# Where 36 weight loads are unpacked in an attention and mixer kernel: eight per head pair in the first batch instead of six, four instead of twelve in the second, and the tail's gap in a shared tile

## The chip, the cores and the metric

The kernel runs on one core of one Trainium2 chip. The metric is device time in microseconds: the median of three runs, 1661.66 us (1660.54 to 1661.77). One further execution was taken by the hardware profiler; all rows come from it.

A core has a matrix engine (TensorE, PE in the profile; PEld is its weight load), a vector engine (VectorE, DVE), an activation engine (ScalarE, ACT), a general engine (GpSimd, POOL) and a queue that issues transfers (SyncE, SP). Each engine works through its own instructions in order and waits on semaphores for the others.

## What is computed

```python
B, H, S, D = 8, 8, 576, 64;  top_k = 32
scores = q @ k^T / sqrt(D)                  # per head, 576 x 576
kth    = the 32nd largest score of each row
scores = where(scores >= kth, scores, -1e9)
attn   = softmax(scores);  o = attn @ v
x  = o laid out as (B, S, 512)
xt = x.transpose(0, 2, 1)                   # mixer, low rank 32
u  = x + (xt @ U @ V).transpose(0, 2, 1)
out = u + relu(u @ w_ch1) @ w_ch2           # 512 -> 2048 -> 512
```

q, k and v are float32. U, V, w_ch1 and w_ch2 come in as float64. The kernel reads them as pairs of 32-bit words and makes float32 of them on the chip.

## The kernel before

**Steps.** Eight batches of four head pairs each. The 576 rows of a pair are four tiles of 128 and a tail of 64 rows, with both heads of the tail in one tile. In the first batch (pairs g = 0 to 3) the tail is a step of its own, so a pair has five steps, t = 0 to 4. From pair 4 on (`NPAIR` = 4) the tail shares the step of t = 3, and a pair has four steps. That makes 20 + 28 × 4 = 132 steps, numbered n; `ALONE` = 20 is the first step of the second batch.

**What one step does.** `scores` multiplies q and k on PE (L350) and ScalarE copies the result to SBUF, into the tile `Ssb` or, for a tail, `Stail` (L395, L404 to L406, L415, L418). `front` finds the 32 largest of each row on VectorE with four rounds of MAX8 and MATCH_REPLACE8 (L521, L534, L539). From pair 5 on, `fold` and `split` first sort each row's two halves into the larger and the smaller of two scores, with two POOL operations (L446, L449) and one of VectorE (L448), so that VectorE handles half the width; L448 needs the copied scores of the next step, and L502, L500 of the next step need L449.

Then scores below the 32nd are pushed down. A "pooled" lane does it with two POOL operations (L544, L545). A "gap" lane does it with ScalarE and POOL: L565 scales the 32nd largest, L571 writes max(0, (32nd − score) × 2^96) into a tile, and POOL subtracts this from the scores (L572). In the second and later batches a step has two gap lanes, and the step with the tail three, written in the order head 1, head 0, tail. ScalarE then takes the exponential and its row sum (L453; L582 finishes the sums).

The probabilities are transposed, by PE (`turns`, L634, L639, with copies L635, L640) for pairs 0 to 5 and by VectorE with a transfer through DRAM (`blocks`, L598, and `back`, L613) from pair 6 on. `values` multiplies them with v (L708, L711, L682) and ScalarE copies the result (L720). `mixed` scales and mixes a finished pair with U and V on PE (L750, L761, L773, L785), POOL writing the result uT (L740, L743, L801).

**The order of the work.** It is written out by hand in the loop over n, as calls of generators; no scheduler moves anything. `fill` emits matmuls of the running batch's two dense layers (`mlp`, L845 and L862, with ScalarE evictions L857 and L873) by a budget per call, so PE does the layers of one batch during the attention of the next. Each batch's layers begin when its last pair is mixed, those of batch 0 at step 20. The last batch's layers are done at the end by a multiplication scheme with fewer products (`closing`).

**The weights.** `params` lists 36 pieces: four for U and V, 16 for w_ch1, 16 for w_ch2. `next_params(1)` moves a three-stage pipeline by one: it emits the ScalarE passes still outstanding, joins the piece before last, splits the last piece, and issues the transfer of the next one (L157 on SP, 512 KB, into one of three `raw` buffers). A split queues three ScalarE passes (L179, L180, L183), of which each `fill` emits one. A join (`f64_join`) is one shift on VectorE and two additions on POOL (L203, L205). The shift is of one of two forms: the plain one with one input (L202), or, if fewer than `LATE` pieces were left when the piece was split, one with two tensor inputs (L193).

In the first batch `next_params(1)` stands in the middle of steps t = 0, 1, 2 and at the end of steps t = 0, 1, 3. From step 21 on it stands near the beginning of every step, and in the middle of steps t = 0, 1, 2. Step 19 has none, step 20 one.

**Tiles and buffers.** The pool `attn` gives a tile by tag, with a number of buffers: asking for a tile means waiting until the use of the buffer's previous tile is over. Tag `E` has two buffers; it holds the gaps of heads 1 and 0 and the POOL mask of the pooled lane. Tag `tplace` has one buffer; it holds the work copy of the tail's scores in the rounds and, in the kernel before, the tail's gap.

Line numbers below are those of the profile of the kernel before.

Of the kernel before, what the change touches and what calls it, by code (L numbers as in the profile page):

```python
# [8 lines left out]
F32 = mybir.dt.float32  # L9
# [17 lines left out]
def kernel(  # L27
# [29 lines left out]
    B, H, S, D = q.shape  # L57
    P = 128
# [4 lines left out]
    NT, TAIL = 4, 64  # L63
# [3 lines left out]
    NPAIR = H // 2  # L67
# [15 lines left out]
    attn = ctx.enter_context(tc.tile_pool(name="attn", bufs=2))  # L83
# [56 lines left out]
        return slice(h * D, (h + 1) * D)  # L140

    SLAB = 512
    LATE = 12
    spare = []


# [13 lines left out]
    def f64_parts(raw, out):  # L160
# [23 lines left out]
        ))  # L184
        return hi, bits, low, len(params) < LATE

    def f64_join(hi, bits, low, late, outs):

        if late:
            none = nought if len(bits.shape) == 2 else nought.rearrange("p o -> p o ()")
            nc.vector.scalar_tensor_tensor(  # L193
                out=bits,
                in0=bits,
                scalar=3,
                in1=none.to_broadcast(list(bits.shape)),
                op0=ALU.logical_shift_left,
                op1=ALU.bitwise_or,
            )  # L200
        else:
            nc.vector.tensor_single_scalar(bits, bits, 3, ALU.logical_shift_left)  # L202
        nc.gpsimd.tensor_tensor(bits, bits, hi, ALU.add)  # L203
        for dst, form in outs:
            nc.gpsimd.tensor_tensor(dst.bitcast(U32), form(bits), form(low), ALU.add)  # L205
# [26 lines left out]
    def next_params(n):  # L232

        while passes:
            passes.pop(0)()
        while parts:
            f64_join(*parts.pop(0))
        while raws:
            r, outs = raws.pop(0)
            if isinstance(outs, list):  # L240
                parts.append((*f64_parts(r, None), outs))
                continue
            made = f64_parts(r, outs)
            parts.append((*made, [(made[1], same)]))
        for _ in range(min(n, len(params))):
            srcs, outs = params.pop()
            raws.append((f64_raw(srcs), outs))
# [6 lines left out]
    def load(g):  # L254

        list(loading(g))
# [211 lines left out]
    def front(tiles):  # L468
# [72 lines left out]
        for c, chunk, total, _, way in lanes:  # L541
            if way == "pooled":
                gap = attn.tile([P, S], F32, tag="E", name="E")
# [17 lines left out]
        if gaps:  # L561
            slots = [lane[0] for lane in gaps]
            lo, hi = min(slots), max(slots) + 1
            least = small.tile([P, 3], F32, tag="least", name="least", bufs=3)
            nc.scalar.mul(least[:, lo:hi], m8[:, lo:hi, 7], WIDEN)  # L565
            for c, chunk, *_ in gaps:
                if c == 2:
                    gap = attn.tile([P, S], F32, tag="tplace", name="E", bufs=1)
                else:
                    gap = attn.tile([P, S], F32, tag="E", name="E")  # L570
                nc.scalar.activation(gap, chunk, AF.Relu, bias=least[:, c : c + 1], scale=-WIDEN)  # L571
                nc.gpsimd.tensor_tensor(chunk, chunk, gap, ALU.subtract)  # L572
            yield
# [593 lines left out]
    def fill(k=1):  # L1167


        nonlocal due  # L1170
        for _ in range(k):
            if passes:
                passes.pop(0)()
            if mixing and next(mixing[0], True):
                mixing.pop(0)
            due += share * (LONG if len(tiles(n)) > 1 else 1) * (EARLY if n <= ALONE + BATCH + 2 else 1)
            while due > 0:
                if not fillers:
                    due = 0.0
                    break  # L1180
                done = next(fillers[0], None)
                if done is None:
                    fillers.pop(0)
                elif not done:
                    due = 0.0
                else:
                    due -= done
# [24 lines left out]
    t = 0  # L1212
# [5 lines left out]
    for n in range(STEPS + 2):  # L1218
        if n < STEPS:
            g, t = steps[n][0]  # L1220
            if t == 0 and g < NPAIR:
                load(g + 1)
            if t == (1 if g < NPAIR else 2) and g + 1 < NP:
                ready = prep(g + 1)
            fronts[n] = front(steps[n])
            next(fronts[n])
        else:
            t = NT
        here, last = fronts.get(n, iter(())), fronts.pop(n - 1, iter(()))
        if n >= ALONE - 1 and n <= ALONE:  # L1230

            if n < ALONE:
                next(last)
                values(*steps[n - 3][0])
                list(turning)
                next(here)
                next(last)
                scores(*steps[n + 1][0])
                fold(*steps[n + 1][0])
                values(*steps[n - 2][0])  # L1240
            list(turns(*steps[n - 1][0]))
            values(*steps[n - 1][0])
            if n < ALONE:
                split(*steps[n + 1][0])
                next(here)
                next(here)
                inverse(g, 0, 2 * NT)
                mixing.append(mixed(g, 1))
                fill()
                next(here)  # L1250
                continue
            fill()
            scores(*steps[n + 1][0])
            fold(*steps[n + 1][0])
            next(here)
            while mixing:
                fill()
            next_params(1)
            fill()
            next(last, None)  # L1260
            next(here)
            fill()
            split(*steps[n + 1][0])
            next(here)
            coming = loading(g + 1)
            next(coming)
            next(coming)
            next(here)
            fill()
            continue  # L1270
        if n < ALONE:
            ease = n > 0 and eased(*steps[n - 1][0])
            if ease:
                next(last, None)
            scores(*steps[n + 1][0])
            fold(*steps[n + 1][0])
            if n >= 3:
                values(*steps[n - 3][0])
                if (n - 3) % CH == NT:
                    mixing.append(mixed((n - 3) // CH, 3))  # L1280
            list(turning)
            fill()
            next(here)
            if t < NT - 1:
                next_params(1)
            fill()
            next(ready, None)
            next(here)
            next(last, None)
            fill()  # L1290
            split(*steps[n + 1][0])
            next(here)
            if t in (0, 1, NT - 1):
                next_params(1)
            next(here)
            fill()
            if n >= 1:
                turning = turns(*steps[n - 1][0])
            continue
        next(last, None)  # L1300
        fill()
        if ALONE <= n - 3 <= STEPS - 3:
            weighted(n - 3)
            if waiting:
                waiting.clear()
                if next(mixing[0], True):
                    mixing.pop(0)
        for tile_ in tiles(n + 1):
            if tile_[1] < NT:
                scores(*tile_, len(tiles(n + 1)) > 1)  # L1310
            fold(*tile_)
        next_params(1)
        turn()
        fill()
        turn()
        next(last, None)
        for tile_ in tiles(n - 2):
            back(*tile_)
        fill()
        turn()  # L1320
        fill()
        next(last, None)
        if n < STEPS and n - 2 >= ALONE and len(tiles(n - 2)) > 1:
            scale(steps[n - 2][0][0])
        next(here, None)
        fill()
        if n >= STEPS:
            if n == STEPS:
                inverse(NP - 1, 0, 2 * NT + 1)
                scale(NP - 1)  # L1330
            weighted(n - 2)
        next(here, None)
        for tile_ in tiles(n + 1):
            split(*tile_)
        if t < NT - 1:
            next_params(1)
        fill()
        next(here, None)
        for tile_ in tiles(n - 1):
            if shared(*tile_):  # L1340
                blocks(*tile_)
        turning = turned(n - 1)
        if n < STEPS and n - 1 >= ALONE and len(tiles(n - 1)) > 1:
            inverse(steps[n - 1][0][0], 0, 2 * NT + 1)
        if n < STEPS:
            if t == NT - 1:
                coming = loading(g + 2) if g + 2 < NP else iter(())
            next(coming, None)
        next(ready, None)
        next(here, None)  # L1350
        fill()
        fill()
# [35 lines left out]
```

## Time and profile before

| | |
|---|---|
| median of three runs | 1661.66 us |
| profiled execution | 1663.47 us, its span 1661.4 us |
| PE busy | 1562.3 us (94%) |
| VectorE busy | 1550.0 us (93%) |
| ScalarE busy | 991.2 us (60%) |
| POOL busy | 1012.4 us (61%) |
| mean granted PE clock | 0.966 |
| plain shifts L202, late shifts L193 | 24 from 20.9 to 203.5 us; 12 from 210.7 to 290.7 us |

A page of the profile lists busy time by engine, the span in slices, the chain of work that ended last, and groups of instructions by source line with the idle time before them and what ended it. Answers of the trace give the same for a stretch, and single instructions in order of time. A name such as `uT<-up` reads "tile uT, written from tile up". A busy PE need not be a PE at its peak, since matmuls overlap and their ends are modelled. Where a wait has several causes, the one that came last is named.

The first batch takes the first 199 us. Step 23, the first with a tail, ends at 250 us on VectorE; its step is the longest, 18.7 us, since pair 4 is not folded.

### The profile page before, as it was taken

Reading aid. Unit: us, or ns where it says so; the run is one execution under the profiler, and the core shown is the slowest. Engines: PE = TensorE matmul, PEld = TensorE weight load, DVE = VectorE, ACT = ScalarE, POOL = GpSimd, SP = SyncE. Lnnn points to the kernel's source line nnn. Section 1 sums busy time; section 2 is a strip of 40 time slices with the busy share of each in tenths; the row PEclk is TensorE's granted clock in tenths of the full one; section 3 lists DMA queues with packets and bytes.
Section 4 is the critical chain, followed back from the end, with each engine's and each line's share of the span. In section 5 each row is a group of like instructions: output and inputs, shape, how many; then the busy total and the mean of one; then the engine's idle time right before and its main releaser. Section 6 shows DMA issues by size and latency. Waiting matters only on the chain.

```text
span 1661.4 us, 30244 instructions
## 1 busy us (share of the span) xinstructions
PE 1562.3 (94%) x9638; PEld 1188.0 (72%) x9638; DVE 1550.0 (93%) x4394; ACT 991.2 (60%) x2475; POOL 1012.4 (61%) x881
## 2 busy tenths in 40 slices
PE   4676698999899999999999999999999999999999
PEld 2444466787677887778777887788777877788776
DVE  7999999999999999999999999999999999994452
ACT  4888778665555666566665656566665656564320
POOL 4787669666656565666666565656666565653620
PEclk7777798999999999999999999999999999999999
DMA  3323232244545555454445555454545455543001
GB/s 88 90 82 94 67 95 74 57 128 128 136 126 140 139 144 138 133 138 131 129 130 137 132 152 133 131 138 129 131 128 140 129 154 132 134 123 110 8 2 29
DMA packets 280399, 189.42 MB, mean 114 GB/s; under 512 B 174288, under 2 KB 261168, under 8 KB 280240
## 3 DMA queue, kind: packets, MB, share of 16 engines
q1 hardware_dynamic: 259728, 117.62, 29.3%
q10 hardware_dynamic: 20512, 69.87, 13.3%
q8 instruction: 76, 1.25, 0.3%
q14 instruction: 83, 0.68, 0.1%
HBM read 116.49 MB, written 70.91 MB: 113 GB/s over the span
## 4 chain that ended last, share of the span: by engine, by line
PE 69%; DVE 20%; DMA 3%; POOL 3%; ACT 2%; SPq 2%; issue 1%; ACTq 0%; DVEq 0%; POOLq 0%
PE mm L862 22%; PE mm L845 19%; DVE m L539 7%; PE sc L350 6%; DVE upper L534 6%; PE O L711 6%; PE mm L938 3%; DVE first L521 2%; PE tp L938 2%; PE sc L938 2%; PE sc L382 2%; PE up L785 2%; DVE y L598 1%; PE O L708 1%; DVE place L534 1%
## 5 line engine op out<-in xcount | busy, mean ns | idle before, releaser
L845 PE MATMUL mm<-uT,w 128*128 128x320 f32 (+1 forms) x1792 | 465.3, 411 | 3.0 <-POOL uT L801 2.3
L862 PE MATMUL mm<-hT,w 128*128 128x320 f32 (+1 forms) x1792 | 462.0, 409 | 0.0
L572 POOL TENSOR_TENSOR Ssb<-Ssb,E 128x576 f32<-128x576 f32 x243 | 341.3, 1424 | 195.2 <-ACT E L571 195.2
L845 PEld LDWEIGHTS mm<-uT,w 128*128 128x128 f32 x1792 | 335.7, 192 | 104.2 <-issue 12.8
L862 PEld LDWEIGHTS mm<-hT,w 128*128 128x128 f32 x1792 | 333.6, 191 | 92.6 <-issue 11.1
L539 DVE MAX8 m<-upper 128x8 f32<-128x304 f32 (+1 forms) x774 | 362.7, 509 | 0.7
L534 DVE MATCH_REPLACE8 upper<-m,upper 128x304 f32<-128x304 f32 (+1 forms) x516 | 256.8, 505 | 0.0
L446 POOL TENSOR_TENSOR lower<-Ssb 128x576 uint32<-128x576 uint32 x108 | 152.8, 1415 | 133.3 <-ACT Ssb L395 71.3
L449 POOL TENSOR_TENSOR lower<-lower,upper 128x576 uint32<-128x576 uint32 x108 | 152.3, 1410 | 130.2 <-DVE upper L448 128.0
L453 ACT ACTIVATE Ssb<-Ssb,nmax 128x576 f32<-128x576 f32 x258 | 201.7, 784 | 19.4 <-POOL Ssb L545 9.8
L350 PE MATMUL sc<-qkT 64*128 64x288 f32 (+1 forms) x1056 | 177.7, 459 | 9.8 <-ACT Ssb L404 7.9
L571 ACT ACTIVATE E<-Ssb,least 128x576 f32<-128x576 f32 x243 | 176.2, 768 | 4.3
L502 DVE MAX8 upper<-lower 128x8 f32<-128x288 f32 x432 | 172.0, 439 | 4.4 <-POOL lower L449 4.4
L395 ACT COPY Ssb<-sc 128x576 f32<-128x576 f32 x216 | 127.5, 642 | 75.7 <-PE sc L350 75.7
L598 DVE STREAM_TRANSPOSE y<-Ssb 128x512 f32<-128x512 f32 (+1 forms) x312 | 154.1, 545 | 0.3 <-ACT Ssb L453 0.2
L711 PE MATMUL O<-PT,va 128*64 128x128 f32 x2048 | 143.8, 284 | 0.0
L857 ACT ACTIVATE hT<-mm 128x320 f32<-128x320 f32 (+1 forms) x224 | 91.1, 408 | 81.7 <-PE mm L845 77.5
L350 PEld LDWEIGHTS sc<-qkT 64*128 64x128 f32 (+1 forms) x1056 | 95.7, 197 | 50.1 <-issue 17.5
L711 PEld LDWEIGHTS O<-PT,va 128*64 128x64 f32 x2048 | 112.6, 140 | 16.1 <-issue 1.6
L720 ACT COPY XT<-O 128x128 f32<-128x128 f32 x128 | 34.0, 266 | 113.1 <-PE O L711 108.3
L534 DVE MATCH_REPLACE8 upper<-first,upper 128x304 f32<-128x304 f32 x216 | 97.5, 459 | 0.0
L500 DVE MATCH_REPLACE8 lower<-upper,lower 128x288 f32<-128x288 f32 x216 | 94.0, 443 | 0.0
(268 smaller groups left out, 2271.6 us busy)
## 6 DMA issues: line engine op xcount, KB each, us to landing
away<-y SPq DMA_DIRECT2D x416, 144.0 KB
PT<-away ACTq DMA_DIRECT2D x104, 576.0 KB
raw<-in_moe_w_ch_dram SPq DMA_DIRECT2D x32, 512.0 KB
va<-in_v_dram SPq DMA_DIRECT2D x64, 128.0 KB
scale<-rd ACTq DMA_DIRECT2D x56, 144.0 KB
out_dram<-ob SPq DMA_DIRECT2D x59, 128.0 KB
ld<-in_q_dram SPq DMA_DIRECT2D x108, 64.0 KB
ld<-in_k_dram SPq DMA_DIRECT2D x108, 64.0 KB
```

Source lines behind the costliest of these rows:

```text
L350: nc.tensor.matmul(out, lhsT=qkT[half(h), 0, cols(t)], rhs=qkT[half(h), 1, lo:hi], start=True, stop=True,)
L446: nc.gpsimd.tensor_tensor(bottom, a.bitcast(U32), b.bitcast(U32), ALU.add)
L453: nc.scalar.activation(E, chunk, AF.Exp, bias=nmax, scale=SCALE, accum_out=total)
L502: nc.vector.max(spot, lower)
L534: nc.vector.match_replace(nxt, ms[c], curs[c], NEG)
L539: nc.vector.max(ms[c], curs[c])
L571: nc.scalar.activation(gap, chunk, AF.Relu, bias=least[:, c : c + 1], scale=-WIDEN)
L572: nc.gpsimd.tensor_tensor(chunk, chunk, gap, ALU.subtract)
L598: nc.vector.transpose(y[:, :, i * NT : i * NT + c].rearrange("p r c j -> p c r j"), E2[:, a : a + c * P].rearrange("p (c r j) -> p c r j", ...
L711: nc.tensor.matmul(O[half(h)], lhsT=va[:, h, j, :], rhs=PT[:, NT * h + j], start=False, stop=(j == NT - 1),)
L845: nc.tensor.matmul(phs[f][:, 0:w], lhsT=first_layer(cc, f), rhs=uT[:, cc, lo:hi], start=(cc == 0), stop=(cc == NC - 1),)
L862: nc.tensor.matmul(po[:, 0:w], lhsT=w2[:, f, c * P : (c + 1) * P], rhs=hTs[f][:, 0:w], start=(f == 0), stop=(f == NF - 1),)
```

## The change

Three things change. In the first batch `next_params(1)` stands at the end of every step and no longer only of t = 0, 1, 3, which makes eight calls a pair instead of six. In the second batch the calls are at other places of a step: one after the second round of maxima, left out in step 23 (`border`), and one at the end of the step, before the gaps of its lanes are emitted. With `LATE` = 4 only the last four pieces take the two-input shift. And the tail's gap is written to a tile of tag `E` like the others.

```diff
-    LATE = 12
+    LATE = 4
...
             for c, chunk, *_ in gaps:
-                if c == 2:
-                    gap = attn.tile([P, S], F32, tag="tplace", name="E", bufs=1)
-                else:
-                    gap = attn.tile([P, S], F32, tag="E", name="E")
+                gap = attn.tile([P, S], F32, tag="E", name="E")
                 nc.scalar.activation(gap, chunk, AF.Relu, bias=least[:, c : c + 1], scale=-WIDEN)
                 nc.gpsimd.tensor_tensor(chunk, chunk, gap, ALU.subtract)
...
             split(*steps[n + 1][0])
             next(here)
-            if t in (0, 1, NT - 1):
-                next_params(1)
+            next_params(1)
             next(here)
             fill()
...
             fold(*tile_)
-        next_params(1)
         turn()
...
         next(here, None)
+        border = g == NPAIR and t == NT - 1
+        if not border:
+            next_params(1)
         fill()
...
             split(*tile_)
-        if t < NT - 1:
-            next_params(1)
         fill()
...
         next(ready, None)
+        if t != 0 or g == NPAIR + 1:
+            next_params(1)
         next(here, None)
```

In numbers: 30 pieces instead of 23 are joined in steps 0 to 19, six in both kernels in steps 20 to 23, and none instead of seven in steps 24 to 27. PE executes the same instructions in the same order.

## The prediction

> **What bounds the kernel now.** I read the chain that ended last, then the stretches of ten and fifty microseconds, then the timelines of single engines where two stretches differ. Steps are the loop's 132 iterations: 0 to 19 are the first batch, five to a pair; from 20 on a pair has four.
>
> ```profile
> PE 69%; DVE 20%; DMA 3%; POOL 3%; ACT 2%; SPq 2%; issue 1%; ACTq 0%; DVEq 0%; POOLq 0%
> ```
>
> TensorE carries the end and VectorE the start. The stretches (from:to, length, busy of PE, PEld, DVE, ACT, POOL, granted clock, DMA share, GB/s) show where they change places:
>
> ```profile
> 50.00:100.00 50.00, 33.93 (x216) 22.80 (x216) 49.59 (x104) 40.44 (x96) 39.54 (x28) 0.76 0.31 88
> ...
> 250.00:260.00 10.00, 7.04 (x20) 4.93 (x21) 10.00 (x31) 9.85 (x24) 8.74 (x6) 0.66 0.00 0
> 260.00:270.00 10.00, 9.84 (x62) 7.04 (x62) 9.42 (x29) 9.97 (x23) 9.92 (x8) 1.00 0.45 127
> 270.00:280.00 10.00, 10.00 (x90) 7.73 (x89) 9.09 (x29) 8.51 (x20) 9.84 (x8) 1.00 0.59 174
> 280.00:290.00 10.00, 7.50 (x25) 4.64 (x24) 8.21 (x22) 7.26 (x17) 9.69 (x11) 0.83 0.02 5
> 290.00:300.00 10.00, 10.00 (x71) 7.33 (x70) 10.00 (x28) 5.82 (x16) 9.60 (x9) 1.00 0.00 0
> ...
> 320.00:330.00 10.00, 10.00 (x87) 7.57 (x86) 8.54 (x27) 4.95 (x15) 3.45 (x3) 1.00 0.46 121
> ```
>
> In the first batch VectorE alone is full. After 250 us POOL, then PE is, and VectorE waits. VectorE's waits between 200 and 345 us, in us and times, name whom it waits for:
>
> ```profile
> DVE upper L502 <- POOL lower L449: 3.7, 4, 1.8
> DVE upper L448 <- ACT Stail L415: 2.1, 1, 2.1
> ```
>
> The first is POOL late with parameter work (steps 25 to 27). The second, at step 30, is PE late: the copies wait for its scores, which end at 329.87. PE has two gaps before that (timeline: start, length, what, idle before it and releaser):
>
> ```profile
> 247.54 1.24 PE L845 MATMUL mm<-uT,w 128*128 128x320 f32 x4
> 252.96 1.11 PE L634 MATMUL tp<-ident,Ssb 128*128 128x128 f32 x4 [4.18 <-ACT XT L720]
> ...
> 284.18 0.44 PE L750 MATMUL tp<-ident,uT 128*128 128x128 f32 x2 [2.01 <-POOL uT L740]
> ...
> 285.75 4.36 PE L862 MATMUL mm<-hT,w 128*128 128x320 f32 x10
> ```
>
> So the path is VectorE to 250, PE to 331, then VectorE again: it shows no wait above 0.1 us from step 31 to 39, while PE idles 6 us between 402 and 435. Beyond that both are full; a group of four steps takes 46.5 us (step 48 begins at 539.56, step 52 at 586.03).
>
> **The change, part by part.** Eight parameters per pair: the calls at the ends of t = 2 and t = 4 are new. By the order of instructions, 30 instead of 23 parameters are joined in the first batch, 6 as before in steps 20 to 23, none instead of 7 in steps 24 to 27; the eight whose shift was late become the plain shift. PE's order is unchanged.
>
> *Seven more shifts in the first batch* lie on full VectorE. What a shift costs depends on POOL:
>
> ```profile
> 77.42 0.85 DVE L202 TENSOR_SCALAR w<-w 128x512 uint32<-128x512 uint32 x1
> ...
> 82.37 0.40 DVE L202 TENSOR_SCALAR w<-w 128x512 uint32<-128x512 uint32 x1
> ...
> 210.69 1.75 DVE L193 SCALAR_TENSOR_TENSOR w<-w,nought 128x512 uint32<-128x512 uint32 x1
> ...
> 269.98 0.68 DVE L193 SCALAR_TENSOR_TENSOR w<-w,nought 128x512 uint32<-128x512 uint32 x1
> ```
>
> From start to next start the plain shift takes 0.32 us, and 0.75 to 0.77 in 4 of 24 cases, each behind a POOL tensor-tensor in flight (at 77.42 L205, 76.69 to 77.99); it is then the rest of that plus some 0.27. At the seven new places (ends of steps 2, 4, 7, 9, 12, 14, 17) such an operation is in flight each time: L545 with 0.8 us left at 57.1, 103.9 and 150.7, L203 or L205 with under 0.2 left at the others. So 3 × 1.0 + 4 × 0.45 = 4.8 us; the rows bound it by 7 × 0.32 = 2.3 and 7 × 0.77 = 5.4. The GPSIMD Engine Reference of the Trainium skill (Key points) says that POOL shares its SBUF interfaces with VectorE, and contends with its two-port and two-input forms. The rows at 71.54 and 82.37, shifts of 0.41 and 0.40 us during POOL's L544, do not show that for every POOL operation; by the page alone all seven would cost the higher price.
>
> Their 21 ScalarE passes (0.67 to 0.77 us each) and 14 POOL additions (1.29 us each) I cost at nothing: the copies VectorE needs are 3 to 8 us early at steps 1 to 19, and POOL's idle stretches of 3.5 us before the join at the end of t = 3 and 1.9 and 2.1 us in t = 0 take a pair of 2.6. If that cover is gone VectorE stands up to 2.6 us, three times or more: 0 to 8. SP gains seven loads; the q and k loads behind them are issued at 143 for transposes at 164, so they have room. The exception is step 20, whose copies are early by 0.4 only: one more 0.77 us pass before them (end of step 18) gives +0.4 (0 to 2.6, if POOL's pair is also in the way).
>
> *Steps 20 to 23*: before, five late shifts stand 1.67, 0.74, 0.60, 0.60 and 1.28 = 4.9 us on VectorE before its last maximum at 250.06. After, beside the plain shift at 203 that both have, one plain and three late ones; by what POOL should be doing at their new places (L572 in flight at the first and third), 0.95, 0.60, 1.2, 0.60 = 3.35, so −1.5 (all free: −2.8; all waiting: +1).
>
> *The end of step 23.* The last late shift now stands behind that maximum, and its two POOL additions ahead of step 23's gap subtractions:
>
> ```profile
> 250.09 0.21 ACT L565 ACTIVATE least<-m 128x3 f32<-128x3 f32 x1 [7.07 <-DVE m L539]
> 250.32 1.44 ACT L571 ACTIVATE E<-Ssb,least 128x576 f32<-128x576 f32 x2
> 251.67 0.76 ACT L571 ACTIVATE E<-Stail,least 128x576 f32<-128x576 f32 x1
> ...
> 252.65 0.25 ACT L720 COPY XT<-O 128x128 f32<-128x128 f32 x1
> ```
>
> POOL begins L572 at 251.18. With shift (0.6), L203 and L205 first it begins at 253.4: +2.2. The tail's gap now takes the E tile of the step's first gap (two buffers), so ScalarE must wait for that first subtraction: by old times 252.59 instead of 251.67, +0.95. Behind it queue L857, L720 and the copies, and PE waits for L720. PE's gap grows by 2.2 + 0.95 = 3.2 us. Without POOL's part it is 0.95; nothing makes it a gain. The clock in 250 to 260 is 0.66; half speed lasts until 258.1, five us after PE resumes. A longer gap may add a stretch of 3.4 us at half speed, 0 to 1.7: I take 0.7.
>
> *Steps 24 to 27*: without parameters POOL has uT ready before PE asks: PE's idle at 284 (2.01 + 0.26 + 0.22 = 2.5) goes. Half speed after it goes as well: ten matmuls took 4.15 us in the chain, eighteen later 4.85, so 10 × 0.27 = 2.7 against 4.15, 1.5 us. Together −4.0 (−2.5 if the clock falls anyway). The Trainium skill's page TensorE: Matmul & The Clock Gate (The HAM clock gate) wants a full idle window of about 3.4 us for half rate. Here 2.5 us of gaps were followed by it, so the row decides; by the page the 1.5 would not hang on this gap, and the sum would be 1.5 us worse.
>
> VectorE loses seven late shifts (1.39 + 0.60 + 1.37 + 0.60 + 1.36 + 0.60 + 1.51 = 7.4 us) and 3.25 us of waits for L449. I cost this at nothing: PE is full from 285 to 331, and scores for step 31 end when it gets there. VectorE, early, stands longer at L448.
>
> *The tail's gap* later: 26 more times ScalarE waits 0.96 us. At 491 the copies behind it are wanted by POOL (L446) only at 494.74, and ScalarE idles 2.67 us soon after. Where a hidden-layer eviction is next (444.7, 537.6, 631.3), PE wants its bank 0.83 to 1.47 us later. Nothing, 0 to 0.4 each.
>
> Sum: 4.8 + 0.4 − 1.5 + 3.2 + 0.7 − 4.0 = +3.6 us. The profiled execution took 1663.47 us at a span of 1661.4, 1.8 above the median of the three runs, 1661.66; put on the median this is 1665.3.
>
> **The rivals.** *PE is not the bound in steps 24 to 31.* Then VectorE's 10.7 us come back: 4.8 + 0.4 − 1.5 − 10.7 = −7.0, 1654.7; it ends on the other side. It decides if VectorE's stand at L448 of step 30 does not grow. For it: VectorE waited 3.25 us for POOL. Against: PE is 10.00 of 10 from 290 on.
> *The prices are at their lower ends*: 2.3 in the first batch, 0.95 at 253: 2.3 − 1.5 + 0.95 − 2.5 = −0.8, 1660.9, no measurable change. For it: 20 of 24 plain shifts were free of POOL.
> *The first batch backs up*: POOL at 39.54 of 50 gets 5.2 us more per pair, ScalarE (40.44) 4.4; exponentials already wait for L545. If VectorE stands 2.6 us once per pair, 3.6 + 7.8 = +11.4, 1673.1.
> *The E tile bites later too*: 0.3 us each in the 12 groups where an eviction follows, +3.6 more, 1668.9.
>
> **How the numbers follow.** No change means within 0.2%, 3.3 us, about what a measurement of this kernel can tell from none. Forecast 0.45, of which 0.28 above 3.3 us and 0.17 below; lower ends 0.25 (0.15 no change, 0.10 faster); PE not the bound 0.10; backing up 0.15; E tile later 0.05. Slower 0.48, same 0.32, faster 0.20. Leaving out half of the fastest and slowest cases: 1657 to 1672; the slower cases alone: 1663 to 1672.
>
> **What would show it.** Right: 30 plain shifts before step 20, step 20 beginning 4 to 6 us later; PE's gap near 253 about 7 us; none at uT; VectorE's wait at L448 of steps 26 to 30 above 5 us in sum. Wrong: VectorE idle in steps 5 to 19 (backing up), L448's waits no longer than 2 us (PE not the bound), or PE gaps at evictions in the later groups.

## The result and the profile after

| | before | after |
|---|---|---|
| median of five runs | 1661.44 us (1660.54 to 1661.77) | 1667.77 us (1666.82 to 1668.06) |
| ratio after to before | | 1.0038, 95% interval 1.0023 to 1.0052 |
| profiled execution | 1663.47 us, span 1661.4 | 1667.81 us, span 1665.6 |
| step 20 begins | 199.13 us | 207.51 us |
| last maximum of step 23 ends | 250.06 us | 257.50 us |
| PE resumes after it | 252.96 us | 263.51 us |
| step 32 begins | 353.70 us | 358.60 us |
| step 131 begins | 1501.76 us | 1506.00 us |

The changed kernel is slower by 0.38%, 6.3 us. The time is inside the range, 2.5 us above the predicted 1665.3. From step 32 to step 131 the two kernels keep the same pace within 0.7 us; the change is made before that.

In the profile of the changed kernel the lines after L567 stand three lower than before (L569 is the gap subtraction that was L572, L717 was L720). The chain that ended last:

```profile
PE 65%; DVE 25%; DMA 4%; SPq 2%; issue 1%; POOL 1%; ACT 1%; ACTq 0%; DVEq 0%; POOLq 0%
```

VectorE's share rose from 20% to 25%: the stretch that VectorE carries has grown. The stretches of the changed kernel (columns as in the prediction):

```profile
50.00:100.00 50.00, 32.27 (x198) 21.67 (x196) 49.73 (x101) 42.78 (x100) 43.58 (x31) 0.77 0.34 103
250.00:260.00 10.00, 6.90 (x45) 4.67 (x43) 10.00 (x23) 2.09 (x4) 3.18 (x3) 1.00 0.00 0
260.00:270.00 10.00, 6.49 (x20) 4.63 (x21) 7.46 (x26) 7.11 (x19) 7.67 (x6) 0.66 0.00 0
270.00:280.00 10.00, 10.00 (x63) 7.39 (x62) 10.00 (x36) 7.86 (x19) 5.62 (x4) 1.00 0.30 57
280.00:290.00 10.00, 10.00 (x90) 7.64 (x90) 7.31 (x25) 5.29 (x14) 5.59 (x6) 1.00 0.14 37
290.00:300.00 10.00, 10.00 (x68) 7.20 (x67) 8.97 (x27) 6.10 (x15) 6.80 (x7) 1.00 0.01 2
```

In the first batch VectorE is full as before and POOL rose by 4 us in 50. From 270 on PE is full and VectorE is not. VectorE's waits from 200 to 350 us, in us, times and longest:

```profile
DVE upper L448 <- ACT Stail L415: 4.8, 2, 2.7
DVE upright L648 <- ACT den L579: 4.2, 2, 2.4
DVE upper L502 <- POOL lower L449: 1.5, 2, 1.0
```

VectorE now waits for ScalarE, at L448 for its copies of PE's scores and at L648 for its sums, and little for POOL. From 245 to 345 us PE itself has one gap left, and none before uT (timeline of PE):

```profile
263.51 0.48 PE L631 MATMUL tp<-ident,Ssb 128*128 128x128 f32 x1 [6.61 <-ACT XT L717]
...
291.60 0.60 PE L747 MATMUL tp<-ident,uT 128*128 128x128 f32 x4
292.03 0.27 PE L758 MATMUL tp<-ident,uT 128*64 128x128 f32 x1
292.14 2.86 PE L859 MATMUL mm<-hT,w 128*128 128x320 f32 x10
```

The ten matmuls after uT take 2.86 us; before, they took 4.36 at half speed. PE executes the same matmuls in the same order in both kernels, so each has a delay against its counterpart of before. It is 10.55 us at the first matmul after the gap (263.51 against 252.96), 9.65 when the clock is full again, 6.5 behind the transposes of uT, 5.07 ten matmuls later, and so to step 32.

**Where the first batch lost 8.4 us.** VectorE idles no more there than before: 0.3 us in each tail step in both kernels. The seven new shifts take from start to next start 0.35, 1.08, 0.37, 1.07, 0.37, 1.09 and 0.37: 4.7 us. The rest is in shifts that both kernels have. Those in the middle of t = 0 (steps 5, 10, 15) take 1.42 instead of 0.32 each, 3.3 in all, and one at 79.96 takes 1.09 instead of 0.77. The one of step 10, first in the changed kernel, then in the kernel before (timeline):

```profile
110.36 0.67 ACT L179 ACTIVATE w<-raw 128x512 f32<-128x512 f32 x1
...
110.88 1.29 POOL L205 TENSOR_TENSOR w<-w,raw 128x512 uint32<-128x512 uint32 x1
...
111.16 0.77 ACT L568 ACTIVATE E<-Ssb,least 128x576 f32<-128x576 f32 x1
...
112.12 1.41 POOL L569 TENSOR_TENSOR Ssb<-Ssb,E 128x576 f32<-128x576 f32 x1
112.31 1.50 DVE L202 TENSOR_SCALAR w<-w 128x512 uint32<-128x512 uint32 x1
```

```profile
107.10 0.78 ACT L571 ACTIVATE E<-Ssb,least 128x576 f32<-128x576 f32 x1
...
107.95 1.72 POOL L572 TENSOR_TENSOR Ssb<-Ssb,E 128x576 f32<-128x576 f32 x1 [1.88 <-ACT E L571]
108.00 0.40 DVE L202 TENSOR_SCALAR w<-w 128x512 uint32<-128x512 uint32 x1
```

Before, the shift began 0.05 us after POOL's subtraction and was free. After, it begins 0.19 us after it and ends with it. The page SBUF — State Buffer of the Trainium skill (SBUF: two separate sides) says that VectorE, in its two-port or two-input forms, and GpSimd share a pair of ports under an exclusive lock, which the one that begins first keeps for its whole instruction. No row names the form of the shift; its times agree with such a lock. At 112.31 the shift's end, 113.81, is 0.28 us behind POOL's at 113.53. At 108.00 it is POOL's operation that is longer, 1.72 against 1.41, although by the recorded starts POOL began 0.05 us earlier: which of the two is first can't be read from starts that lie so close.

### The profile page after: what moved, and what is told of

Same layout as the page of the kernel before. It is cut to its first block, busy times and chain, and to the rows that moved or that the text cites. A ratio compares the mean times of both kernels' runs of the same rounds, so it can differ in the third digit from the quotient of the medians.

```text
span 1665.6 us, 30249 instructions
## 1 busy us (share of the span) xinstructions
PE 1559.5 (94%) x9638; PEld 1183.5 (71%) x9638; DVE 1551.1 (93%) x4394; ACT 992.2 (60%) x2475; POOL 1009.5 (61%) x881
## 3 DMA queue, kind: packets, MB, share of 16 engines
q8 instruction: 76, 1.25, 0.3%
## 4 chain that ended last, share of the span: by engine, by line
PE 65%; DVE 25%; DMA 4%; SPq 2%; issue 1%; POOL 1%; ACT 1%; ACTq 0%; DVEq 0%; POOLq 0%
PE mm L859 20%; PE mm L842 19%; DVE m L539 8%; DVE upper L534 7%; PE sc L350 6%; PE O L708 5%; PE mm L935 3%; DVE first L521 3%; DMA PT<-away 2%; DVE y L595 2%; PE tp L935 2%; PE sc L935 2%; PE sc L382 2%; DVE place L534 1%; PE up L782 1%
## 5 line engine op out<-in xcount | busy, mean ns | idle before, releaser
L569 POOL TENSOR_TENSOR Ssb<-Ssb,E 128x576 f32<-128x576 f32 x243 | 339.8, 1419 | 183.3 <-ACT E L568 183.3
L717 ACT COPY XT<-O 128x128 f32<-128x128 f32 x128 | 33.9, 265 | 95.9 <-PE O L708 91.8
```

## The experiments

Each time is the median of several runs, each ratio is to the kernel before on the same chip, with its 95% interval. The kernel before had a median of 1662.26 us beside the first four kernels that were measured (first batch alone, own tile, middle of t = 3, three things mended), 1661.31 beside the next four (the three with additions or shifts taken away and seven calls) and 1661.56 beside the last four; differences from the changed kernel go by the ratios. Step starts are those of the profiled execution.

### One part of the change at a time

**The first batch's part alone** (L numbers of before):

```diff
-    LATE = 12
+    LATE = 4
...
-            if t in (0, 1, NT - 1):
-                next_params(1)
+            next_params(1)
             next(here)
```

> The kernel before with eight calls per pair in the first batch and LATE = 4; the calls of the second batch stay at their old places and the tail keeps its own gap tile. Theory (the first batch costs 8.4 us, 4.7 by the seven new shifts and 3.6 by old shifts in the middle of t = 0 that now meet POOL; steps 24 to 27 give back 4.0; the end of step 23 costs 3.1 through the new places): step 20 begins at 207.5 instead of 199.1, PE's gap near 262 is about 4.2 us as before, PE does not idle for uT; 8.4 - 0.5 - 4.0 = +3.9, about 1665.3 us, some 2.5 us under the changed kernel. Rival (the first batch carries all and the second batch's places nothing): as the changed kernel, 1667.8 us. Rival (the new shifts cost only the 4.8 that were forecast): step 20 at 203.9, 1661.7 us.

Measured: 1665.83 us, 1.0021 (1.0013 to 1.0030), some 3.5 us over the kernel before. Step 20 begins at 207.48, the same as with the whole change; PE's gap is 4.16 us, as it was before; there is none for uT, and PE's delay falls from 8.2 at 253 to 2.1 behind uT. So the later start of step 20 comes from the first batch's calls alone, and the places in the second batch and the tile cost the other 2.8 us.

**The tail's gap in its own tile again**, else the changed kernel:

```diff
             for c, chunk, *_ in gaps:
-                gap = attn.tile([P, S], F32, tag="E", name="E")
+                if c == 2:
+                    gap = attn.tile([P, S], F32, tag="tplace", name="E", bufs=1)
+                else:
+                    gap = attn.tile([P, S], F32, tag="E", name="E")
```

> The changed kernel with the tail's gap back in a tile of its own (tag tplace), all else kept. Theory (the shared tile costs one wait, at the end of step 23, and nothing later): ScalarE does not wait for POOL before the tail's gap of step 23, PE's gap near 263 falls from 6.6 to about 5.6 us, 0.95 us under the changed kernel: 1666.8 us. Rival (the tile bites in later groups too): 4 to 8 us less. Rival (POOL alone sets that gap): no difference, 1667.8 us.

Measured: 1664.13 us, 1.0014 (1.0005 to 1.0022): 4 us under the changed kernel, four times the 0.95 expected. The profiled execution, 1662.37 us, is the fastest of twelve. The end of step 23, in the changed kernel (POOL and ScalarE, timeline):

```profile
258.15 1.29 POOL L203 TENSOR_TENSOR w<-w,raw 128x512 uint32<-128x512 uint32 x1 [3.28 <-DVE w L193]
...
259.53 1.28 POOL L205 TENSOR_TENSOR w<-w,raw 128x512 uint32<-128x512 uint32 x1
...
260.76 2.77 POOL L569 TENSOR_TENSOR Ssb<-Ssb,E 128x576 f32<-128x576 f32 x2
...
262.20 0.78 ACT L568 ACTIVATE E<-Stail,least 128x576 f32<-128x576 f32 x1 [3.00 <-POOL Ssb L569]
...
263.20 0.26 ACT L717 COPY XT<-O 128x128 f32<-128x128 f32 x1
```

And with the tail's own tile:

```profile
256.94 1.29 POOL L203 TENSOR_TENSOR w<-w,raw 128x512 uint32<-128x512 uint32 x1 [3.28 <-DVE w L193]
...
257.90 0.76 ACT L568 ACTIVATE E<-Stail,least 128x576 f32<-128x576 f32 x1
...
258.31 1.30 POOL L205 TENSOR_TENSOR w<-w,raw 128x512 uint32<-128x512 uint32 x1
...
258.88 0.25 ACT L717 COPY XT<-O 128x128 f32<-128x128 f32 x1
...
259.18 0.66 PE L631 MATMUL tp<-ident,Ssb 128*128 128x128 f32 x4 [2.49 <-ACT XT L717]
```

POOL's two additions stand ahead of the subtractions here too, and POOL's subtractions begin as late after the last maximum. ScalarE no longer waits for them: it writes the tail's gap at 257.90, and the copy L717 that PE wants follows. PE resumes 2.89 us after the last maximum (256.29), as in the kernel before (2.90). PE's delay at that place falls by 4.3, a part of which is a shift of step 20 that was free in this execution (0.32 instead of 1.12). The clock does not fall after the gap either.

**The call at the end of step 23 left out**, the shared tile kept:

```diff
-        if t != 0 or g == NPAIR + 1:
+        if (t != 0 or g == NPAIR + 1) and not border:
             next_params(1)
```

> The changed kernel, without the call at the end of step 23 (its join falls in step 24), the tail's gap still in the shared tile. Theory (POOL's two additions reach PE only through the shared tile: ScalarE waits for the first subtraction, and that stands behind them): ScalarE's wait falls from 3.0 to about 0.9 us, PE's gap near 262 from 6.6 to about 4 us, 1664.5 to 1665.3 us. Rival (the two additions are a term of their own beside the tile's): the gap falls by 2.2 and is 0.95 above that of the kernel with its own tile, which then would have kept the 2.2, 5.5 us or more; its 2.5 us speak against it already.

Measured: 1665.60 us, 1.0024 (1.0015 to 1.0034), about 2 us under the changed kernel. ScalarE's wait for the tail's gap is 0.85 us and PE's gap 4.45:

```profile
259.92 0.78 ACT L571 ACTIVATE E<-Stail,least 128x576 f32<-128x576 f32 x1 [0.85 <-POOL Ssb L572]
...
261.22 1.11 PE L634 MATMUL tp<-ident,Ssb 128*128 128x128 f32 x4 [4.45 <-ACT XT L720]
```

**The shared tile alone**, put into the kernel before:

```diff
             for c, chunk, *_ in gaps:
-                if c == 2:
-                    gap = attn.tile([P, S], F32, tag="tplace", name="E", bufs=1)
-                else:
-                    gap = attn.tile([P, S], F32, tag="E", name="E")
+                gap = attn.tile([P, S], F32, tag="E", name="E")
```

> The kernel before with the tail's gap in the shared tile and nothing else. Theory: ScalarE waits 0.95 us in step 23, PE's gap near 253 is 5.1 instead of 4.2 us, and nothing changes later: 0.9 us more, not to be told from no change. Rival (the tile bites in the later groups as well): 4 us more or above, with PE gaps at evictions after 440.

Measured: 1660.89 us, 0.9998 (0.9989 to 1.0006): no change. PE's gap is 5.13 us instead of 4.18, as expected. It is paid back at once: PE comes to uT later and idles 1.11 us there instead of 2.01. Later PE gaps are those of the kernel before.

These three kernels, with the one before and the changed one, make a table of the time from the last maximum of step 23 to PE's next matmul:

| us from maximum to PE | no POOL additions between | additions between |
|---|---|---|
| own tile | 2.90 (before) | 2.89 |
| shared tile | 3.86 and 3.86 | 6.01 (after) |

The additions alone cost nothing, the shared tile alone 0.96, and both together 3.1. The two entries of 3.86 are the kernel without the call at the end of step 23 and the kernel before with the shared tile.

### Where the first batch lost more than its new shifts

**POOL's additions at t = 4 taken away** (edit in `f64_join`, n is the running step):

```diff
+        if n in (4, 9, 14):
+            return
         nc.gpsimd.tensor_tensor(bits, bits, hi, ALU.add)
```

> The changed kernel, but POOL's two additions of the three joins at the end of t = 4 (steps 4, 9, 14) are left out; their shifts stay. Three pieces of the weights are therefore not finished. Theory (the old shift in the middle of t = 0 meets POOL only because those additions put the tail's gap subtraction off): the shifts at 62.7, 112.3 and 161.6 take 0.32 instead of 1.42 us each, step 20 begins at 204.2 instead of 207.5, the time is 3.3 us less, 1664 to 1664.5. Rival (they are slow for another reason, such as the added ScalarE passes or loads): they keep 1.42 us, and the time stays.

Measured: 1668.81 us, 1.0038 (1.0025 to 1.0050): nothing gained. The shifts in the middle of t = 0 take 1.29, 1.30 and 1.31 us instead of 1.42. My first theory, that the additions put the subtraction off and so caused the collision, falls. The 0.5 us that the run gained up to step 15 it lost in step 19, where VectorE idles 0.67 us (0.31 in the changed kernel) while PE runs at half speed from 201 to 208; in steps 20 and 21 it idles another 1.37 us. The same place in this kernel (line numbers two to five higher):

```profile
109.97 0.67 ACT L179 ACTIVATE w<-raw 128x512 f32<-128x512 f32 x1
...
111.61 1.40 POOL L574 TENSOR_TENSOR Ssb<-Ssb,E 128x576 f32<-128x576 f32 x1 [2.45 <-ACT E L573]
111.92 1.38 DVE L202 TENSOR_SCALAR w<-w 128x512 uint32<-128x512 uint32 x1
```

POOL had been idle for 2.45 us and waited for ScalarE's gap, and ahead of that stands the pass L179 of the new piece, which holds ScalarE for 0.58 us (next start at 110.55).

**A shift alone at t = 4**, in the kernel before, without additions, passes or load:

```diff
             if t in (0, 1, NT - 1):
                 next_params(1)
+            if n in (4, 9, 14):
+                nc.vector.tensor_single_scalar(w2_last_piece, w1_first_piece, 3, ALU.logical_shift_left)
             next(here)
```

The piece that it writes is not in use yet, the one that it reads is joined; both are 128x512.

> The kernel before with one more plain shift of 128x512 on VectorE at the end of steps 4, 9 and 14, that computes nothing wanted: no POOL addition, no ScalarE pass, no load goes with it. Theory (VectorE alone is pushed late against POOL, so that its old shift in the middle of t = 0, which began within 0.05 us of POOL's subtraction and was free, now begins inside it): the added shift costs 1.07 us, the old one 1.3 instead of 0.32, 2.05 us per pair and 6.1 us in three, step 20 at 205.3, 1667.5 us. Rival (the old shift is slow through the additions, passes or loads of the new pieces): only the three added shifts, 3.2 us, step 20 at 202.3, 1664.5 us.

Measured: 1665.87 us, 1.0025 (1.0014 to 1.0035), step 20 at 203.08. Steps 1 to 20 take 182.35 us instead of 178.13: 4.2 us for three shifts, between the two expectations.

```profile
105.04 1.08 DVE L1296 TENSOR_SCALAR w<-w 128x512 uint32<-128x512 uint32 x1
...
109.26 1.41 POOL L572 TENSOR_TENSOR Ssb<-Ssb,E 128x576 f32<-128x576 f32 x1 [1.88 <-ACT E L571]
...
110.14 0.80 DVE L202 TENSOR_SCALAR w<-w 128x512 uint32<-128x512 uint32 x1
```

The added shift pushes VectorE by 1.0 us, ScalarE's and POOL's work of the tail stays where it was, and the old shift comes 0.88 us after the subtraction's start instead of 0.05. It then waits for the rest, 0.73 us instead of 0.32. So the 1.1 us that each old shift lost can be set out in three parts: 0.4 from VectorE being pushed, which this run shows; 0.12 from POOL's additions, which leaving them out shows; and 0.57 between the two. For these the rows give ScalarE's pass of 0.58 us before the gap: the subtraction starts later, and the shift meets its beginning instead of its end. No run took the pass alone away, and the two kernels compared differ in the loads and in the calls at t = 2 as well, so this part is read off and not isolated. All of it is one thing, two engines' moments against each other.

**The call of t = 4 in the middle of t = 3**, else the changed kernel:

```diff
-            if t < NT - 1:
+            if t < NT - 1 or (t == NT - 1 and g < NPAIR - 1):
                 next_params(1)
...
             next(here)
-            next_params(1)
+            if t < NT:
+                next_params(1)
             next(here)
```

> The changed kernel, its three first-batch calls at the end of t = 4 moved to the middle of the step before (t = 3). The number of pieces joined before step 20 is the same. Theory (collisions by place): the moved shift comes during POOL's one-tensor L544 and takes 0.32 instead of 1.07; the shift in the middle of t = 0 is free of POOL again, 0.32 instead of 1.42; the shift at the end of t = 3 meets the moved pair of additions, 0.8 instead of 0.32. That is 1.3 us less per pair, 4 us in three pairs: step 20 at 203.5, 1663.8 us. Rival (POOL and VectorE are simply fuller, places do not matter): as the changed kernel, step 20 at 207 to 208, 1667 to 1668 us.

Measured: 1666.19 us, 1.0023 (1.0014 to 1.0033). Step 20 begins at 205.8: 1.7 us earlier, not 4. The shift in the middle of t = 0 is free again (0.32), but the moved shift itself meets the beginning of POOL's L544 and takes 0.66 instead of the 0.32 expected, and the shift at the end of t = 3 meets the moved additions and takes 1.43 instead of 0.8:

```profile
143.32 2.22 POOL L544 TENSOR_SCALAR E<-Ssb,m 128x576 f32<-128x576 f32 x1
...
143.62 0.74 DVE L202 TENSOR_SCALAR w<-w 128x512 uint32<-128x512 uint32 x1
...
149.75 1.30 POOL L205 TENSOR_TENSOR w<-w,raw 128x512 uint32<-128x512 uint32 x1
149.83 1.51 DVE L202 TENSOR_SCALAR w<-w 128x512 uint32<-128x512 uint32 x1
```

**The call in the middle of t = 0 one round later**, else the changed kernel:

```diff
-            if t < NT - 1:
+            if t < NT - 1 and (t or not n):
                 next_params(1)
             fill()
             next(ready, None)
             next(here)
+            if n and not t:
+                next_params(1)
```

> The changed kernel; in the first batch the call in the middle of t = 0 stands one round of maxima later (not in step 0). Nothing is left out. Theory (the shift there is slow only because it comes 0.17 to 0.2 us after the tail's gap subtraction has begun on POOL, L569 at 62.48, 112.12 and 161.46, and that is over 1.4 us later): the shifts of steps 5, 10 and 15 take 0.32 instead of 1.42 us, step 20 begins 3.3 us earlier, at 204.2, about 1664.5 us. Rival (POOL is fuller, the price comes back at the next shift): step 20 at 207 to 208, 1667 to 1668 us.

Measured: 1666.73 us, 1.0031 (1.0019 to 1.0044). The shift of t = 0 takes 0.32 us, and the next one 1.25 to 1.27 instead of 0.32:

```profile
114.63 0.40 DVE L202 TENSOR_SCALAR w<-w 128x512 uint32<-128x512 uint32 x1
...
117.56 1.31 POOL L205 TENSOR_TENSOR w<-w,raw 128x512 uint32<-128x512 uint32 x1
...
117.82 1.34 DVE L202 TENSOR_SCALAR w<-w 128x512 uint32<-128x512 uint32 x1
```

Steps 1 to 20 take 186.2 instead of 186.5 us. Two attempts to move one collision have thus ended in another: here the rival was right in effect, with eight joins a pair the price comes back, although each price hangs on a place.

### What bounds steps 24 to 31

**POOL's additions of steps 24 to 27 taken away**, in the kernel before:

```diff
+        if 24 <= n < 28:
+            return
         nc.gpsimd.tensor_tensor(bits, bits, hi, ALU.add)
```

> The kernel before, POOL's two additions of the seven joins in steps 24 to 27 left out, their shifts kept; seven pieces of the weights are not finished. Theory (PE is the bound from 285 to 331 and the 4 us were PE's wait for uT and the clock after it, both by POOL): PE has no gap before uT's transposes near 284 and no half speed after it, 4 us less, about 1658.3. Rival (VectorE is the bound there): only the part of 3.25 us that VectorE waits for POOL and what its shifts wait for POOL (some 3 us) come back, 1656, with VectorE not idle at L448.

Measured: 1657.58 us, 0.9975 (0.9966 to 0.9985), 3.7 us less. PE has no gap before uT's transposes and no half speed after them; its gain is 2.4 us at 284 and 4.7 us behind. VectorE has no wait in steps 24 to 28 either, so this run does not tell the two apart.

**VectorE's shifts of steps 24 to 27 taken away**, in the kernel before:

```diff
-        if late:
+        if 24 <= n < 28:
+            pass
+        elif late:
```

> The kernel before, the seven VectorE shifts of the joins in steps 24 to 27 left out (7.4 us of VectorE), POOL's additions kept; seven pieces of the weights are not finished. Theory (PE is the bound there): nothing, 0 to -1 us, and VectorE stands up to 7 us longer at L448 and L449. Rival (VectorE is the bound): 7 us less, about 1655.

Measured: 1659.01 us, 0.9983 (0.9974 to 0.9992): 2.3 us less, more than the 0 to 1 expected and far from the rival's 7. The gain is PE's: its idle time before uT falls from 2.5 to 0.67 us (1.8), where POOL's additions have no shift to wait for, and no half speed follows (1.4 more in the profiles). The rest of the 7.4 us bought nothing; VectorE waits longer for POOL, 6.4 us instead of 3.7, and at L448 (here L450) the same 2.1:

```profile
DVE upper L504 <- POOL lower L451: 6.4, 4, 3.6
DVE upper L450 <- ACT Stail L417: 2.1, 1, 2.1
```

### Two versions put together from this

**Three things mended**: the call of t = 4 in the middle of t = 3, the own tile, no call at the end of step 23 (the three diffs above).

> The changed kernel with three things mended together: the call of t = 4 in the middle of t = 3, the tail's gap in its own tile, and no call at the end of step 23 (the last join then falls in step 24, after the second round). Theory: 4.0 + 0.95 + 2.2 = 7.2 us under the changed kernel, 1660.6 us, and PE's gap near 259 back at about 4.2 us. Rival (what is saved at the end of step 23 is lost again before step 31, since PE then waits somewhere else): 4 us under it, 1663.8 us.

Measured: 1662.35 us, 1.0001 (0.9992 to 1.0010), as fast as the kernel before, and some 6 us under the changed kernel where 7.2 were expected. The end of step 23 is mended: PE resumes 2.91 us after the last maximum, and its gap is 2.54 us, not the 4.2 expected, since PE's work before it ends later; the first batch gains 1.9 us instead of 4, as in the run that moved the call alone.

**Seven calls a pair**: as the last one, but no call in the first batch at t = 4 and none in the middle of t = 3:

```diff
             next(here)
-            next_params(1)
+            if t < NT:
+                next_params(1)
             next(here)
```

> Seven calls per pair in the first batch (the end of t = 2 added, none at t = 4), 27 pieces joined there; the second batch's places as in the changed kernel but none at the end of step 23; the tail's gap in its own tile. The last four pieces are joined in steps 24 and 25. Theory (the call at t = 4 is what made the first batch dear; the end of t = 2 costs 0.37 us each, and one join after it 0.3 more): step 20 begins near 200.9, steps 24 to 31 give back some 4 us, 1657 to 1658 us, faster than both kernels. Rival (four joins left in steps 24 and 25 put uT off again as they did before): 1661 to 1662, no better than the kernel before.

Measured: 1658.46 us, 0.9979 (0.9970 to 0.9988): faster than the changed kernel, and than the one before by 0.2%. Steps 1 to 20 take 179.6 us, 1.5 more than before for four new shifts of 0.34 to 0.37. The shift in the middle of t = 0 stays free:

```profile
155.77 0.41 DVE L202 TENSOR_SCALAR w<-w 128x512 uint32<-128x512 uint32 x1
155.81 1.64 POOL L569 TENSOR_TENSOR Ssb<-Ssb,E 128x576 f32<-128x576 f32 x1 [1.88 <-ACT E L568]
```

It begins 0.04 us ahead of POOL. PE does not wait for uT, although four joins are left in steps 24 and 25.

## Why the prediction was right, and where not

Slower, by an amount inside the range: the direction held. But part of that is luck. The sum was 2.7 us short of the 6.3, and 3.6 us of what was measured stand in a term that the prediction does not have; without these the change would have cost, by this estimate, 6.3 − 3.6 = 2.7 us, which the prediction itself counts as no change (within 3.3). Its terms were off in both directions. In the profiles:

| term | predicted | measured | from |
|---|---|---|---|
| seven new shifts | +4.8 | +4.7 | their rows |
| old shifts of the first batch | none | +3.6 | 3 × 1.10 and 0.32 |
| start of step 20 | +0.4 | 0 and +0.8 | copies; shift at 211.87 |
| steps 20 to 23 | −1.5 | −1.7 | 8.38 + 0.80 − 1.75 = 7.4 at the last maximum |
| end of step 23 | +3.2 | +3.1 | 10.55 − 7.44 |
| clock behind it | +0.7 | −0.9 | 9.65 − 10.55 |
| steps 24 to 27 | −4.0 | −4.6 | 5.07 − 9.65 |
| VectorE in 24 to 27, later gaps | 0 | 0 | |
| sum | +3.6 | +5.0 | +4.9 at step 32, +4.2 at the end |

**The step that failed** is "Seven more shifts in the first batch": it priced the new shifts, to 0.1 us in sum, and did not ask what the old ones would meet once VectorE, ScalarE and POOL stood otherwise against each other. The rows were there: the old shifts of t = 0 stood within 0.05 us of a POOL subtraction and were counted among the free ones. "Backs up" was the wrong rival for it: VectorE idles no more than before in steps 5 to 19; the loss is inside its busy time. The rule behind the price, the rest of POOL's operation plus some 0.27, mixes two measures: from start to next start it is 0.21 more than the rest, and 0.28 is how long the shift's own row runs past POOL's. The mark "step 20 beginning 4 to 6 us later" is missed with 8.4.

**The start of step 20**: the copies were no later than before. The 0.8 us there is again a collision, with POOL's L755 begun 0.13 us earlier; in five of the kernels above L755 began up to 0.31 us after the shift, which then took 0.32. Whether they meet changes without any change here: the kernel without POOL's late additions is the kernel before up to step 24, and in its profile the same shift took 0.96 us, L755 having begun 0.28 us earlier.

**Steps 20 to 23** came out by two misses that cancel: the first shift met more of POOL's subtraction than expected (1.35 us at 222.64 instead of 0.95), the third missed it (0.62 at 234.24 instead of 1.2).

**The end of step 23** is right in its sum and in its shape with both causes present, wrong in what each cause is. It added 2.2 for POOL's additions to 0.95 for the tile. The runs show that the two work only together: ScalarE's queue, and PE behind it, see POOL's delay only through the shared tile. Without the shared tile the 2.2 would not have existed.

**The clock**: the term had the wrong sign. Half speed lasted 6.8 us in both profiles, but in the changed kernel PE resumed later in it: 3.9 us of it were left (267.4 − 263.51) and before 5.1 (258.1 − 252.96). Half of that difference is 0.6 us; the rest of the 0.9 was not traced.

**Steps 24 to 27**: the mechanism stands: PE has no gap before uT in the run without POOL's additions, in the run with the first batch's part alone and in the changed kernel, and a gap of 0.67 without the shifts. The −1.5 does not follow from such a gap alone: the run with the idle shift had the same gaps before uT (1.99, 0.26 and 0.23 us) and no half speed behind them. The profiled execution of before was 2.0 us above its median of five, that of after at its median, so some 2 of the missing 2.7 us are that: the sum was put on the median as if the profile were a typical one.

**The rivals.** "PE not the bound" is refuted by the run without the late shifts; the mark itself, L448's waits above 5 us, came out at 4.8, and another 4.2 us of VectorE's idle time stand at L648. "E tile bites later" is refuted by the shared tile alone. "Prices at their lower ends" did not come: three of the new shifts took 1.07 to 1.09 us.

## What to carry to other kernels

An engine that is full has a price list only for the moments its instructions have now. Moving work by a microsecond on one of two engines that share a port changes what the unmoved instructions meet; look through all of those that stand within some tenths of a microsecond of the other engine's start, and count each as a possible loss, before adding new ones in the same loop. And where two delays are added up at one wait, ask through which buffer or queue each of them reaches it: if it is the same one, they don't add, and taking away either may take away both.

## What the runs showed of the hardware

**A collision hangs on less than 0.1 us.** Shifts that began up to 0.05 us after a two-tensor POOL operation took 0.32 us (at 108.00 before, for one); at 0.08 to 0.09 us (149.83 with the call in the middle of t = 3) and above they took the rest of it plus some 0.2. In all fourteen profiles every plain 128x512 shift that began 0.08 us or more into a two-tensor operation, with over 0.1 us of it left, ended 0.28 to 0.29 us behind it. POOL's one-tensor L544 let shifts pass that came 0.81 us or more after its start (at 74.08 in the changed kernel, 0.92 after it), and two that came 0.07 and 0.08 after it, but not those that came 0.27 to 0.34 after it: these ended 1.02 to 1.04 us after its start in all of five cases. The skill's page on SBUF, cited above, gives the lock for the whole instruction; for L544, 2.2 us long, these rows show only its first microsecond.

**The clock goes by windows.** The half-speed stretches are whole multiples of 3.41 us and lie on a fixed grid of that length within an execution. I added up PE's idle time by such windows from 235 to 490 us in the thirteen profiles that show a change of clock there. In all 23 windows at full clock that were followed by half speed it was 1.74 us or more (in six of them all 3.41), in all that were not 1.65 or less. The same gaps before uT, first in the kernel before (one window), then with the idle shift (split over two); columns as above, the granted clock third from the end:

```profile
281.90:285.40 3.50, 1.14 (x5) 0.41 (x4) 3.31 (x8) 2.37 (x7) 3.42 (x5) 0.99 0.00 0
285.40:288.80 3.40, 3.26 (x7) 2.24 (x8) 1.80 (x7) 2.99 (x6) 3.24 (x4) 0.50 0.00 0
```

```profile
283.30:286.80 3.50, 2.34 (x9) 1.33 (x7) 3.50 (x10) 3.50 (x10) 3.42 (x3) 1.00 0.05 11
286.80:290.20 3.40, 2.07 (x9) 1.31 (x10) 1.86 (x3) 2.30 (x6) 3.25 (x6) 1.00 0.00 0
290.20:293.60 3.40, 3.40 (x35) 2.54 (x33) 3.13 (x11) 1.86 (x5) 3.32 (x4) 1.00 0.02 5
```

In the first, PE is busy 1.14 of 3.5 us and the next window runs at half speed; in the second, 2.34 and 2.07, and it does not. The page TensorE: Matmul & The Clock Gate (The HAM clock gate) says that the window is 3.4 us and free-running, which these stretches agree with, and that it takes an idle window; here about half of one was enough. Where the grid lay against the work differed from profile to profile, so a gap of 2 to 2.5 us cost 1.5 us more in one and nothing in another; two profiles of one kernel, which would show that it differs between executions, are not on record. The later gap of 2.25 us near 438 did so in the profile of before and not in that of after.
